# Causal scores by 64x64 tiles of the PE array, with the state update and the way of x^T moved

## The chip, the cores and the metric

The kernel runs on one core of a Trainium2 chip. The metric is the device time of one execution in microseconds (us), the median of several runs. TensorE (PE) multiplies matrices, VectorE (DVE) and ScalarE (ACT) work element by element, GpSimd (POOL) does the masking, and SyncE (SP) issues the DMA transfers. Matmuls write to PSUM, everything else lives in SBUF.

## What is computed

A gated linear attention (outer-product state with a forget gate) is followed by a multiplicative feed-forward network:

```python
batch, n_heads, seq, head_dim = (4, 8, 768, 48)
n_tokens, d_model, d_ff = (3072, 384, 1024)

f = 1.0 / (1.0 + np.exp(-f_logit))
for t in range(S):
    state = f[:, :, t, :, None] * state + np.einsum('bhd,bhe->bhde', k[:, :, t], v[:, :, t])
    y[:, :, t] = np.einsum('bhd,bhde->bhe', q[:, :, t], state)
x = y.transpose(0, 2, 1, 3).reshape(B * S, H * D)
a = x @ w1
b = x @ w2
out = ((a * b) @ w3) @ w_out
```

All inputs and the output are float32 except the weights, which arrive as 64-bit words and are converted on the chip.

## The kernel before

The sequence is cut into 24 units of 128 tokens (six for each of the four batches), each with all eight heads. For a unit, products of gates are built by scans on VectorE, so that with Q = q times the product of the gates from the unit's start and K = k times its reciprocal, the scores of a head are K^T Q, and everything before the unit comes through a state of 48x48 per head. Heads are stored in pairs: partitions 0 to 47 hold one head of a pair (`par` = 0), partitions 64 to 111 the other, and `hp` counts the four pairs. Six blocks of 512 tokens (four units each) then go through the feed-forward network (FFN). Here w3 and w_out are first folded into one matrix (L999), and the FFN products are made with seven instead of eight block products from the second block on (L542). A scheduler in the kernel (`Plan`) books each task with an estimated cost and emits the instructions of all engines in the order of the plan.

The tasks of one unit that the change touches, cut to their core. The pairs, their way out of PSUM, and the causal mask:

```python
def pairs():
    s["pa"] = ps.tile([P, 2, NQ], F32, name="pa")
    for hp in range(HP):                       # HP = 4, C = P = 128, NQ = 512
        cols = slice(hp * C, hp * C + C)
        for par in range(2):
            nc.tensor.matmul(
                s["pa"][:, par, cols], lhsT=s["K"][rows(par), cols], rhs=s["Q"][rows(par), cols],
                start=True, stop=True,
            )
...
def taken():
    s["A"] = work.tile([P, 2, HP, C], F32, name="A")
    nc.scalar.copy(s["A"].rearrange("p r h c -> p r (h c)"), s["pa"])
...
def causal():
    a = s["A"].rearrange("p r h c -> p (r h) c")
    nc.gpsimd.affine_select(
        out=a, in_=a, pattern=[[0, H], [1, C]], compare_op=ALU.is_ge, fill=0.0, base=0,
        channel_multiplier=-1,
    )
```

The values (scores times v) and, in the same task, what the state gives (queries); the update of the state is a task of its own:

```python
def side(u, hp, par):                          # column half and block of a head's output
    if u < NPE:                                # NPE = 4: the first four units
        return par, hp
    return (par ^ 1 ^ hp & 1), 2 * par + hp // 2
...
def value():
    ...
    for hp in range(HP):
        for par in range(2):
            half, b = side(u, hp, par)
            ...
            nc.tensor.matmul(
                y_block(b)[64 * half : 64 * half + w], lhsT=s["v"][:, h * D : h * D + w],
                rhs=s["A"][:, par, hp], start=bank not in met_, stop=opens, skip_group_check=True,
            )
    if not opens:
        for hp in range(HP):
            ...
            for par in range(2):
                half, b = side(u, hp, par)
                nc.tensor.matmul(
                    y_block(b)[rows(half)], lhsT=sb[(u - 1) % 2][rows(par), hp, rows(par)],
                    rhs=s["Q"][rows(par), hp * C : hp * C + C], start=False, stop=True,
                    skip_group_check=True,
                )
...
def update():
    s["pd"] = ps.tile([P, HP, R], F32, name="pk")[0:R, :, 0:D]
    for hp in range(HP):
        for par in range(2):
            h = 2 * hp + par
            w = 64 if par == 0 else D
            nc.tensor.matmul(
                s["pd"][64 * par : 64 * par + w, hp], lhsT=s["kt"][:, hp, 64 * par : 64 * par + w],
                rhs=s["v"][:, h * D : h * D + D], start=True, stop=True,
            )
```

The output of a unit is copied to `ys` and brought into the layout that the FFN reads (x^T, features on partitions) by transfers from SBUF to SBUF, ten for a unit; the first four units use matmuls with a permutation instead:

```python
def gather():
    for h in range(H):
        half, b = side(u, h // 2, h % 2)
        for r, kc, at_, m in runs(h):
            a = half * 64 + at_
            nc.sync.dma_start(block_xt()[r : r + m, kc, cols], s["ys"][a : a + m, b])
...
t["z"] = t["x"] = moves(6.2, 197, 300, gather, [t["y"]] + before, n0 - 100)
```

`ys` has three buffers, and the transfers wait (`before`) until the block two earlier has been read.

Of the kernel before, what the change touches and what calls it, by code (L numbers as in the profile page):

```python
# [45 lines left out]
P = 128  # L46
C = 128
# [26 lines left out]
class Plan:  # L74


    def __init__(self):
        self.tasks = []
        self.slots = {}

    def slot(self, name, n):
        self.slots[name] = [n, []]

# [10 lines left out]
    def order(self):  # L94
# [5 lines left out]

        def start(t):

            waits = list(t["deps"])
            for name in t["takes"]:
                n, taken = self.slots[name]
                if len(taken) >= n:
                    waits += enders[id(taken[-n])]
            if any(d["end"] is None for d in waits):
                return None
            return max(  # L110
                [free.get(t["eng"], 0.0)] + [d["end"] + (d["lag"] + t["slack"] if d["eng"] != t["eng"] else 0.0) for d in waits]
            )

        while left:
            at, _, _, t = min(
                ((at, t["prio"], t["no"], t) for t in left if (at := start(t)) is not None), key=lambda x: x[:3]
            )
            t["at"], t["end"] = at, at + t["cost"]
            free[t["eng"]] = t["end"]
            for name in t["takes"]:  # L120
                self.slots[name][1].append(t)
            left.remove(t)
            done.append(t)
# [43 lines left out]

def side(u, hp, par):

    if u < NPE:  # L170
        return par, hp
    return (par ^ 1 ^ hp & 1), 2 * par + hp // 2
# [3 lines left out]
def ranged(ctx, tc, q, k, f_logit, v, w1, w2, w3, w_out, out, ident, w12, wc, left):  # L176
# [11 lines left out]
    one = ctx.enter_context(tc.tile_pool(name="one", bufs=1))  # L188
    ps = ctx.enter_context(tc.tile_pool(name="ps", bufs=1, space=PSUM))
    ps_f = ctx.enter_context(tc.tile_pool(name="ps_f", bufs=NF, space=PSUM))  # L190
# [4 lines left out]
    qs, ks, fs = ([keep.tile([R, NQ], F32, name=f"{nm}{i}") for i in range(n)] for nm, n in (("q", 3), ("k", 2), ("f", 2)))  # L195
    sb = [keep.tile([R, HP, R], F32, name=f"sb{i}") for i in range(2)]
# [33 lines left out]
    plan.slot("f", NF)  # L230
    plan.slot("a", 2)
    plan.slot("ab", 4)
    moving = plan.add("PE", 0.0, lambda: None, takes=["ab"], prio=-1e9)
    coming = plan.add("PE", 0.0, lambda: None, takes=["ab"], prio=-1e9)

    def idle(n):

        to = ps_f.tile([P, TB], F32, name="f")[:, 0:TH]
        for _ in range(n):
            nc.tensor.matmul(to, lhsT=floor[:, 0:P], rhs=floor[:, 0:TH], start=True, stop=True)  # L240
# [56 lines left out]
    def moves(issue, size, rate, emit, deps, prio, late=0.0):  # L297

        i = plan.add("SP", issue, emit, deps, prio, lag=0.6)
        return plan.add("DMA", size / rate, lambda: None, [i], prio, lag=1.3 + late)  # L300

    def attention(u):
        s, t = st[u], tk[u]
        opens, closes = u % NCH == 0, u % NCH == NCH - 1
        n0 = need(u)
        slack = 0.8 if u >= NPE else 0.0
# [15 lines left out]
        t["lf"] = moves(0.87, 197, 250, load(fu, f_logit), free(2, "g"), n0 - 30)  # L322
        t["lk"] = moves(0.87, 197, 250, load(ku, k), free(2, "k"), n0 - 29.5)
        t["lq"] = moves(0.87, 197, 250, load(qu, q), free(3, "q"), n0 - 29)

        def load_v():
            s["v"] = at(12288 + NQ, DM) if u == 3 else loads.tile([P, DM], F32, name="vt")
            nc.sync.dma_start(s["v"], v[u])

        t["lv"] = moves(0.45, 197, 320, load_v, [] if u == 3 else past(u, 4 if u in (4, 5, 6) else 3, "v", "s"), n0 - (28.2, 28.2, 28.2, 29.6, 27)[min(u, NPE)])  # L330
# [5 lines left out]
        if not opens:  # L336
            tk[u - 1]["d"]["deps"].append(t["g"])
# [31 lines left out]
        def scale_k():  # L369
            s["K"] = work.tile([R, NQ], F32, name="K")  # L370
            nc.vector.tensor_tensor(s["K"], ku, s["R"], ALU.mult)  # L371

        t["k"] = plan.add("DVE", 0.7, scale_k, [t["r"], t["lk"]] + past(u, 2, "a", "t"), n0)
# [3 lines left out]
        def pairs():  # L377
            s["pa"] = ps.tile([P, 2, NQ], F32, name="pa")
            for hp in range(HP):
                cols = slice(hp * C, hp * C + C)  # L380
                for par in range(2):
# [3 lines left out]
                    )  # L385

        t["a"] = plan.add("PE", 1.1, pairs, [t["q"], t["k"]] + past(u, 1, "y" if u > NPE else "m"), n0 - 1000, slack=slack)

        def taken():
            s["A"] = work.tile([P, 2, HP, C], F32, name="A")  # L390
            nc.scalar.copy(s["A"].rearrange("p r h c -> p r (h c)"), s["pa"])  # L391

        t["m"] = plan.add("ACT", 1.1, taken, [t["a"]] + past(u, 2, "v"), n0)

        def causal():
            a = s["A"].rearrange("p r h c -> p (r h) c")
            nc.gpsimd.affine_select(  # L397
                out=a, in_=a, pattern=[[0, H], [1, C]], compare_op=ALU.is_ge, fill=0.0, base=0,
                channel_multiplier=-1,
            )  # L400

        t["c"] = plan.add("POOL", 1.2, causal, [t["m"]], n0)

        if not closes:
            def turn():
                s["pk"] = ps.tile([P, HP, R], F32, name="pk")
                for hp in range(HP):
                    nc.tensor.transpose(  # L408
                        out=s["pk"][:, hp], in_=s["K"][:, hp * C : hp * C + C], identity=ident[0:R, 0:R]
                    )  # L410

            t["t"] = plan.add("PE", 0.45, turn, [t["k"]] + past(u, 1, "d"), n0 - 999, slack=slack)

# [6 lines left out]
        def value():  # L420
            if u < NPE:
                s["py"] = ps_f.tile([P, HP, C], F32, name="f")[0:R]
            else:
                s["py"] = ps.tile([P, 2, NQ], F32, name="pa")[0:R, :, 0 : 2 * C]
            met_ = set()
            for hp in range(HP):
                for par in range(2):
                    h = 2 * hp + par
                    half, b = side(u, hp, par)
                    w = 64 if half == 0 else D  # L430
                    bank = (half, 0 if u < NPE else par)
                    nc.tensor.matmul(  # L432
                        y_block(b)[64 * half : 64 * half + w], lhsT=s["v"][:, h * D : h * D + w],
                        rhs=s["A"][:, par, hp], start=bank not in met_, stop=opens, skip_group_check=True,
                    )
                    met_.add(bank)
            if not opens:
                for hp in range(HP):
                    if u < NPE:
                        nc.tensor.matmul(  # L440
                            y_block(hp), lhsT=sb[(u - 1) % 2][:, hp], rhs=s["Q"][:, hp * C : hp * C + C],
                            start=False, stop=True, skip_group_check=True,
                        )
                        continue
                    for par in range(2):
                        half, b = side(u, hp, par)
                        nc.tensor.matmul(  # L447
                            y_block(b)[rows(half)], lhsT=sb[(u - 1) % 2][rows(par), hp, rows(par)],
                            rhs=s["Q"][rows(par), hp * C : hp * C + C], start=False, stop=True,
                            skip_group_check=True,  # L450
                        )

        def y_block(b):
            return s["py"][:, b] if u < NPE else s["py"][:, b // 2, b % 2 * C : b % 2 * C + C]

        t["v"] = plan.add(
            "PE", 1.05 if opens else 2.1 if u < NPE else 1.6, value, [t["c"], t["lv"]] + past(u, 1, "y", "b"),
            n0 - 998, takes=["f"] if u < NPE else [], slack=slack,
        )

        if not closes:
            def update():
                s["pd"] = ps.tile([P, HP, R], F32, name="pk")[0:R, :, 0:D]
                for hp in range(HP):
                    for par in range(2):
                        h = 2 * hp + par
                        w = 64 if par == 0 else D
                        nc.tensor.matmul(  # L468
                            s["pd"][64 * par : 64 * par + w, hp], lhsT=s["kt"][:, hp, 64 * par : 64 * par + w],
                            rhs=s["v"][:, h * D : h * D + D], start=True, stop=True,  # L470
                        )

            t["s"] = plan.add("PE", 0.6, update, [t["e"], t["lv"]] + past(u, 1, "d"), n0 - 997, slack=slack)

# [11 lines left out]
            t["d"] = plan.add("DVE", 0.55 if opens else 0.9, state, [t["s"], t["l"]] + past(u, 2, "b"), n0)  # L486
# [7 lines left out]
        def outcome():  # L494
            s["ys"] = work3.tile([R, HP, C], F32, name="ys")
            ys = s["ys"] if u < NPE else s["ys"].rearrange("p (r b) c -> p r (b c)", r=2)
            nc.scalar.activation(ys, s["py"], AF.Copy, accum_out=ysum[:, u : u + 1])  # L497

        t["y"] = plan.add(
            "ACT", 0.8, outcome, [t["v"]] + past(u, 3, "z"), n0 - 10, frees=[t["v"]] if u < NPE else [],  # L500
# [10 lines left out]
        def gather():  # L511
            for h in range(H):
# [909 lines left out]
```

## Time and profile before

| | |
|---|---|
| time, median of 3 runs | 506.15 us (505.76 to 507.29) |
| span of the profiled execution | 502.6 us |
| instructions | 8896 |
| granted TensorE clock, mean share | 0.998 |
| moved by DMA | 46.02 MB, 92 GB/s on average |

The span can be read as stages. The first 35 us bring up the first four units. From 35 to 76 us the first FFN block runs, from 76 to 130 us the eight folds of w3 and w_out beside the attention. From 130 to 345 us attention and FFN alternate on TensorE, and from 345 us on there is only FFN. In the table of the costliest groups of the page, each line gives the source line, engine, operation, output and inputs, tile rows by columns, moving shape, count, busy time and mean duration. The mean duration of a matmul has the length of its pipeline in it, so the cost of a matmul in a stream is the distance from its start to the next one's start.

Busy times of the engines by stage, as the trace gives them for stretches of the span:

```
us            PE busy   DVE busy   ACT busy   DMA share
0:35          35.00     30.85      22.86      0.85
35:76         41.00     38.65      24.82      0.64
76:130        54.00     52.57      27.96      0.47
130:182       52.00     43.84      21.96      0.38
307:345       38.00     18.71      10.54      0.14
375:502      120.88     69.31      11.37      0.08
```

### The profile page before, as it was taken

The numbers are of one execution on the slowest core, as the hardware profiler recorded it, in microseconds if no ns is written. First come the engines' busy times: TensorE is split into PE (matmuls) and PEld (weight loads), VectorE is DVE, ScalarE is ACT, GpSimd is POOL, SyncE is SP. The second block draws the span as 40 slices with busy tenths as digits, with TensorE's granted clock in tenths as the row PEclk, the third lists the DMA queues.
The fourth block names the chain that finished last, engine by engine and source line by source line (L and its number), as shares of the span: only waits on it lengthen the run. The fifth ranks groups of instructions, "written<-read, shape, count | busy, mean of one in ns | idle before, by whom it ended". The sixth has DMA issues, their size and how long they took to land.

```text
span 502.6 us, 8896 instructions
## 1 busy us (share of the span) xinstructions
PE 492.0 (98%) x3378; PEld 411.0 (82%) x3378; DVE 362.7 (72%) x701; ACT 161.6 (32%) x340; POOL 45.3 (9%) x51
## 2 busy tenths in 40 slices
PE   8899999999999999999999999999999999999995
PEld 6788645666798887889888899888889888889994
DVE  7998999999999868876588666445563777664541
ACT  4697455843344344432242112231010101011000
POOL 9210000101100021011111001000000000000000
PEclk9999999999999999999999999999999999999999
DMA  6996477642244434221151001110012100000011
GB/s 181 297 358 218 140 257 259 218 116 61 62 120 118 132 112 134 83 87 47 43 175 31 1 10 46 47 43 2 0 24 61 45 0 1 0 1 0 33 54 47
DMA packets 31027, 46.02 MB, mean 92 GB/s; under 512 B 6656, under 2 KB 20480, under 8 KB 29952
## 3 DMA queue, kind: packets, MB, share of 16 engines
q1 hardware_dynamic: 30976, 45.38, 29.1%
q8 instruction: 28, 0.46, 0.4%
q14 instruction: 23, 0.19, 0.1%
HBM read 36.70 MB, written 4.72 MB: 82 GB/s over the span
## 4 chain that ended last, share of the span: by engine, by line
PE 93%; DVE 3%; issue 1%; POOL 1%; DMA 0%; ACT 0%; SPq 0%; DVEq 0%; ACTq 0%; POOLq 0%
PE f L542 68%; PE f L999 8%; PE pa L382 5%; PE pa L432 4%; PE pk L468 2%; PE pa L447 2%; PE pk L408 2%; PE f L521 1%; DVE fwd L341 1%; DVE bwd L363 1%; PE f L440 1%; PE f L432 1%; DVE K L371 0%; DMA f<-in_f_logit_dram 0%; DVE Q L357 0%
## 5 line engine op out<-in xcount | busy, mean ns | idle before, releaser
L542 PE MATMUL f<-xt,w 128*128 128x256 f32 (+1 forms) x600 | 160.3, 397 | 0.0
L542 PEld LDWEIGHTS f<-xt,w 128*128 128x128 f32 x600 | 112.8, 190 | 25.0 <-issue 10.9
L542 PE MATMUL f<-place 128*128 128x192 f32 (+1 forms) x504 | 114.0, 351 | 0.0
L542 PEld LDWEIGHTS f<-place 128*128 128x128 f32 x504 | 87.4, 190 | 6.3 <-issue 0.6
L397 POOL TENSOR_SCALAR_AFFINE_SELECT A<-A 128x1024 f32<-128x1024 f32 x24 | 34.1, 1420 | 295.0 <-ACT A L391 295.0
L999 PE MATMUL f<-place 128*128 128x384 f32 x128 | 42.9, 490 | 0.0
L542 PE MATMUL f<-xt,place 128*128 128x256 f32 x144 | 37.7, 384 | 0.0
L999 PEld LDWEIGHTS f<-place 128*128 128x128 f32 x128 | 23.8, 190 | 16.0 <-issue 0.5
L645 ACT COPY a<-f 128x256 f32<-128x256 f32 x36 | 13.4, 372 | 70.8 <-PE f L542 56.7
L542 PE MATMUL f<-wc,ab 128*128 128x192 f32 x192 | 35.3, 327 | 0.0
L391 ACT COPY A<-pa 128x1024 f32<-128x1024 f32 x24 | 24.3, 1012 | 27.2 <-PE pa L382 27.2
L341 DVE TENSOR_TENSOR_SCAN fwd<-gate,floor 112x512 f32<-112x512 f32 x24 | 31.0, 1293 | 2.5 <-ACT gate L333 1.7
L542 PEld LDWEIGHTS f<-wc,ab 128*128 128x128 f32 x192 | 32.0, 190 | 0.7 <-issue 0.2
L669 DVE TENSOR_TENSOR place<-f,a 128x256 f32<-128x256 f32 x36 | 15.2, 423 | 21.5 <-PE f L542 21.3
L363 DVE TENSOR_TENSOR_SCAN bwd<-gate,back 112x512 f32<-112x512 f32 x24 | 29.4, 1225 | 0.7
L542 PEld LDWEIGHTS f<-xt,place 128*128 128x128 f32 x144 | 26.5, 189 | 4.0 <-DVE place L669 0.2
L382 PEld LDWEIGHTS pa<-Q,K 48*128 48x128 f32 x384 | 23.3, 187 | 7.4 <-issue 5.8
L382 PE MATMUL pa<-Q,K 48*128 48x128 f32 x384 | 27.9, 285 | 0.0
L357 DVE TENSOR_TENSOR Q<-q,fwd 112x512 f32<-112x512 f32 x23 | 18.7, 812 | 9.5 <-PE pa L447 9.5
L497 ACT ACTIVATE ys<-pa 112x512 f32<-112x512 f32 x20 | 12.0, 598 | 35.6 <-PE pa L447 18.1
L432 PEld LDWEIGHTS pa<-A,vt 128*48 128x48 f32 x320 | 17.1, 129 | 6.8 <-issue 6.1
L935 ACT ACTIVATE place<-place 128x512 f32<-128x512 f32 (+2 forms) x24 | 21.4, 890 | 3.4 <-DVE w L952 2.0
(110 smaller groups left out, 633.5 us busy)
## 6 DMA issues: line engine op xcount, KB each, us to landing
place<-in_w_dram SPq DMA_DIRECT2D x8, 1024.0 KB, 4.9
place<-in_w_dram SPq DMA_DIRECT2D x12, 512.0 KB, 9.5
out_dram<-o SPq DMA_DIRECT2D x24, 192.0 KB, 2.1
q<-in_q_dram SPq DMA_DIRECT2D x46, 96.0 KB, 2.4
vt<-in_v_dram SPq DMA_DIRECT2D x23, 192.0 KB, 2.8
f<-in_f_logit_dram SPq DMA_DIRECT2D x44, 96.0 KB, 2.3
k<-in_k_dram SPq DMA_DIRECT2D x44, 96.0 KB, 2.4
place<-in_w_out_dram SPq DMA_DIRECT2D x4, 768.0 KB, 5.1
```

The costliest lines, as they stand in the source:

```text
L341: nc.vector.tensor_tensor_scan(s["P"], gate[u % 2][:, 0:NQ], floor, 0.0, ALU.mult, ALU.max)
L357: nc.vector.tensor_tensor(s["Q"], qu, s["P"], ALU.mult)
L363: nc.vector.tensor_tensor_scan(s["R"][:, ::-1], gate[u % 2][:, NQ:0:-1], back[:, ::-1], 0.0, ALU.mult, ALU.max)
L382: nc.tensor.matmul(s["pa"][:, par, cols], lhsT=s["K"][rows(par), cols], rhs=s["Q"][rows(par), cols], start=True, stop=True,)
L391: nc.scalar.copy(s["A"].rearrange("p r h c -> p r (h c)"), s["pa"])
L397: nc.gpsimd.affine_select(out=a, in_=a, pattern=[[0, H], [1, C]], compare_op=ALU.is_ge, fill=0.0, base=0, channel_multiplier=-1,)
L432: nc.tensor.matmul(y_block(b)[64 * half : 64 * half + w], lhsT=s["v"][:, h * D : h * D + w], rhs=s["A"][:, par, hp], start=bank not in met ...
L542: nc.tensor.matmul(out_, lhsT=lhs[i], rhs=rhs[i], start=start and i == 0, stop=i == len(lhs) - 1, skip_group_check=True,)
L645: nc.scalar.copy(q["a"], q["X"])
L669: nc.vector.tensor_tensor(ups["u3", k], q["Y"], q["a"], ALU.add)
L935: nc.scalar.activation(m, hi.bitcast(F32), AF.Abs)
L999: nc.tensor.matmul(w3s["p", jc], lhsT=w3s[jc][:, kc * P : kc * P + P], rhs=wos[:, kc], start=(kc == 0), stop=(kc == KF - 1),)
```

## The change

The change does five things. All but the last concern the units from number 4 on.

1. **Pairs by 64x64 tiles.** A key after a query gives a score that the mask removes. Each head's 128x128 scores are now made in two pieces: the 64 early keys against all 128 queries, and the 64 late keys against the 64 late queries; the corner of late keys and early queries is not computed. For the second head pair of each two, the two halves of K are stored swapped, so that four matmuls at a time fall on the four 64x64 tiles of the array. v is loaded with its halves swapped for these heads, in three transfers instead of one; ScalarE copies the scores in three pieces, and GpSimd masks in four.
2. **The update beside the values.** Values, update and queries are one task, in this order, so values and update share one tile shape. The task waits for the turned K, the mask and the state.
3. **x^T by way of memory.** Two transfers write `ys` to a buffer in DRAM, and one reads it back in the layout of the FFN. For this each half of the partitions holds heads 0 to 3 or 4 to 7, and the heads are taken in the order 0, 2, 1, 3 of `hp`.
4. **Transfers in the schedule.** The plan books each transfer by itself and allows eight at a time (`lane`).
5. **PSUM banks.** The five banks of the FFN are given out by the plan to whoever can start earliest, instead of in turn.

The diff, cut to its core:

```diff
-    plan.slot("f", NF)
+    plan.pool("f", NF)
     plan.slot("a", 2)
+    plan.slot("lane", 8)
...
+def heads_of(u):
+    return range(HP) if u < NPE else (0, 2, 1, 3)
 def side(u, hp, par):
     if u < NPE:
         return par, hp
-    return (par ^ 1 ^ hp & 1), 2 * par + hp // 2
+    return hp // 2, 2 * par + hp % 2
...
+    def moves(n, size, rate, emit, deps, prio, late=0.0):
+        for j in range(n):
+            i = plan.add("SP", 0.45, (lambda: None) if j else emit, [d] if j else deps, prio - j * 1e-3, takes=["lane"], lag=0.6)
+            d = i
+            t = plan.add("DMA", size / n / rate, lambda: None, [i], prio - j * 1e-3, lag=1.3 + late, frees=[i])
+        return t
+
+    def loaded(dst, u):
+        if u < NPE:
+            nc.sync.dma_start(dst, v[u])
+            return
+        to, of = (t.rearrange("p (b two m) -> p b two m", two=2, m=2 * D) for t in (dst, v[u]))
+        nc.sync.dma_start(to[:, :, 0], of[:, :, 0])
+        for a in (0, 64):
+            nc.sync.dma_start(to[a : a + 64, :, 1], of[64 - a : P - a, :, 1])
...
+            kk, k_, r_ = (
+                x.rearrange("p (b two h c) -> p b two h c", two=2, h=2, c=C // 2) for x in (s["K"], ku, s["R"])
+            )
+            nc.vector.tensor_tensor(kk[:, :, 0], k_[:, :, 0], r_[:, :, 0], ALU.mult)
+            nc.vector.tensor_tensor(kk[:, :, 1, ::-1], k_[:, :, 1], r_[:, :, 1], ALU.mult)
...
+        for hp in range(0, HP, 2):
+            for late in range(2):
+                for swap in range(2):
+                    a = (hp + swap) * C
+                    h0 = 64 * (late ^ swap)
+                    for par in range(2):
+                        nc.tensor.matmul(
+                            s["pa"][h0 : h0 + 64, par, a + 64 * late : a + C],
+                            lhsT=s["K"][rows(par), a + h0 : a + h0 + 64],
+                            rhs=s["Q"][rows(par), a + 64 * late : a + C], start=True, stop=True,
+                        )
...
+            for p0, p1, f in ((0, P, slice(1, 4, 2)), (0, 64, slice(0, 1)), (64, P, slice(2, 3))):
+                nc.scalar.copy(...[p0:p1, :, f], ...[p0:p1, :, f])
-        t["m"] = plan.add("ACT", 1.1, taken, ...)
+        t["m"] = plan.add("ACT", 1.1 if u < NPE else 1.5, taken, ...)
...
+            for p0, f in ((0, 0), (0, 3), (64, 1), (64, 2)):
+                select(a[p0 : p0 + 64, :, f], [[0, HP], [1, C // 2]])
-        t["c"] = plan.add("POOL", 1.2, causal, [t["m"]], n0)
+        t["c"] = plan.add("POOL", 1.2 if u < NPE else 1.9, causal, [t["m"]], n0)
...
-        t["v"] = plan.add(
-            "PE", 1.05 if opens else 2.1 if u < NPE else 1.6, value, [t["c"], t["lv"]] + past(u, 1, "y", "b"), ...
-            t["s"] = plan.add("PE", 0.6, update, [t["e"], t["lv"]] + past(u, 1, "d"), n0 - 997, slack=slack)
+            t["a"] = plan.add("PE", 1.0, lambda: pairs(u), ...)
+            def value():
+                values(u)
+                if not closes:
+                    update(u)
+                from_state(u)
+            t["v"] = t["s"] = plan.add(
+                "PE", 1.2 + 0.35 * (not closes) + 0.5 * (not opens), value,
+                [t["c"], t["lv"]] + past(u, 0, "e") + past(u, 1, "y", "b", "d"), n0 - 998, slack=0.8,
+            )
...
-        def gather():
-            for h in range(H):
-                half, b = side(u, h // 2, h % 2)
-                for r, kc, at_, m in runs(h):
-                    a = half * 64 + at_
-                    nc.sync.dma_start(block_xt()[r : r + m, kc, cols], s["ys"][a : a + m, b])
+        def written():
+            s["yt"] = dram.tile([DM, C], F32, name="yt")
+            for half in range(2):
+                to = s["yt"][half * DH : half * DH + DH].rearrange("(b d) c -> d b c", d=D)
+                nc.sync.dma_start(to, s["ys"][rows(half)])
+
+        def gathered():
+            nc.sync.dma_start(block_xt()[:, :, cols], s["yt"].rearrange("(k p) c -> p k c", p=P))
...
-            t["z"] = t["x"] = moves(6.2, 197, 300, gather, [t["y"]] + before, n0 - 100)
+            t["z"] = moves(2, 197, 250, written, [t["y"]], n0 - 100)
+            t["x"] = moves(1, 197, 250, gathered, [t["z"]] + before, n0 - 100)
```

## The prediction

> **What bounds the kernel now.** I began with the busy times and the slices of the page.
>
> ```profile
> PE 492.0 (98%) x3378; PEld 411.0 (82%) x3378; DVE 362.7 (72%) x701; ACT 161.6 (32%) x340; POOL 45.3 (9%) x51
> ...
> PE   8899999999999999999999999999999999999995
> ...
> DVE  7998999999999868876588666445563777664541
> ...
> DMA  6996477642244434221151001110012100000011
> ```
>
> TensorE is occupied for 98% of the span, in every slice but the first two and the last. A busy TensorE need not be at its peak, so next came the chain that ended last.
>
> ```profile
> PE 93%; DVE 3%; issue 1%; POOL 1%; DMA 0%; ACT 0%; SPq 0%; DVEq 0%; ACTq 0%; POOLq 0%
> PE f L542 68%; PE f L999 8%; PE pa L382 5%; PE pa L432 4%; PE pk L468 2%; PE pa L447 2%; PE pk L408 2%; PE f L521 1%; DVE fwd L341 1%; DVE bwd L363 1%; PE f L440 1%; PE f L432 1%; DVE K L371 0%; DMA f<-in_f_logit_dram 0%; DVE Q L357 0%
> ```
>
> The other engines hold it only in the first 19 us (the scans of the first units). After 35 us TensorE never starves. I took the start-to-start distances of its single instructions: the FFN and fold matmuls (L542, L999) after 35 us sum to 383 us at their own pace (216 ns for 256 columns, 163 for 192, 323 for 384), and real waits add only four pieces: 0.35 us at 188.5 (values for their mask), 0.29 at 253.1, 0.81 at 375.6 (the final judgement) and 0.61 at 493.3, 2.1 us in all. So time can be had only from what the attention costs TensorE. Its pieces stand in the TensorE timeline; columns are start, length with the pipeline's tail, line, tiles, shape, count (start to start is the cost):
>
> ```profile
> 192.47 1.16 PE L382 MATMUL pa<-Q,K 48*128 48x128 f32 x16
> 193.63 0.70 PE L542 MATMUL f<-xt,place 128*128 128x256 f32 x2
> ...
> 207.82 1.09 PE L432 MATMUL pa<-A,vt 128*48 128x128 f32 x16
> 208.85 0.66 PE L447 MATMUL pa<-Q,sb 48*48 48x128 f32 x16
> 209.43 0.67 PE L468 MATMUL pk<-vt,kt 128*64 128x48 f32 x16
> 210.03 0.70 PE L542 MATMUL f<-xt,place 128*128 128x256 f32 x2
> ```
>
> Pairs cost 1.09 us, values 1.02, queries of the state 0.585, update 0.595. The counts are twice those in the code (8 matmuls of pairs give x16): each f32 matmul is two passes.
>
> And where values and update already stand side by side (a unit that opens a sequence, with no state to query):
>
> ```profile
> 189.07 1.09 PE L432 MATMUL pa<-A,vt 128*48 128x128 f32 x16 [0.19 <-POOL A L397]
> 189.99 0.64 PE L468 MATMUL pk<-vt,kt 128*48 128x48 f32 x16
> 190.55 0.48 PE L542 MATMUL f<-xt,w 128*128 128x256 f32 x1
> ```
>
> Here values take 0.91, update 0.56: the join without a change of tile shape is cheaper by 0.11.
>
> [...] An FFN matmul before pairs or values takes 309 ns to the next start instead of 216 (+93); the first pass in a new shape lasts longer (+30 for values, +20 to 40 for queries, +101 for pairs); the last adds +93; and the FFN matmul after it takes 320 (+104). In the update the 48- and 64-column tiles run at 45 and 58 ns each, out of step.
> [...]
> [...] The change keeps parity as the bank; the 48x48 queries already run four tiles at 109 ns for 128 columns.
> [...] So x^T pays two landings in series; in this trace one takes 1.8 us.
>
> **The change part by part**, for the 20 units from number 4 on; the first four keep their code.
>
> *Pairs.* Eight matmuls (two row tiles, 128 weight columns) become 16 on four 64x64 tiles. For two head pairs: two passes of 128 columns at 109 (as the queries' quads) and two of 64 at about 58 (weight-bound, as the 64-column update). Twice that is 0.67 us; with 0.03 for the first pass and 0.09 to drain, 0.79 against 1.09. But 64 loads and matmuls in 0.67 us are one per 10 ns; the tightest this trace shows is the queries' 32 in 0.436, one per 13.6. At that pace the stream takes 0.87, the piece 1.0, which is also the cost that the new schedule books. I choose the middle, 0.90: 20 x 0.19 = 3.8 us saved (1.8 to 6).
>
> *Values, update, queries.* Now: 17 x 1.61 + 3 x 0.91 + 13 x 0.595 + 3 x 0.564 = 39.5, and three updates stand between two FFN matmuls at 0.2 extra, together 40.1. After, for the 13 middle units: values 0.911, update 8 x 0.058 = 0.464, switch 0.123, queries 0.436, drain 0.093 = 2.03; three opening units 1.475 and four closing ones 1.61 as now: 37.2, a saving of 2.9. Against it stands the new order of heads: the two column halves no longer alternate with each matmul, but go two and two. If the tiles queue deeply enough, that is free; if the second half starts one pass late, it costs 0.11 x 20 = 2.2. The new schedule books 1.2 for values (1.05 before), so I take half: 2.9 - 1.1 = 1.8 us saved.
>
> *Off the path.* ACT copies the scores in three pieces instead of one of 1.01 us: about 0.60 + 0.37 + 0.37 by its 512- and 256-element copies. GpSimd masks in four ops instead of one (1.09 to 2.11, median 1.29): an estimated 1.6 to 2. K is scaled by two DVE ops of 256 (0.42 each) instead of one of 0.70. The way from scores to values grows by about 1 us, DVE by 0.14 us a unit. Units come every 10 us or more and the FFN fills, so this costs nothing unless a wait like that at 188.5 grows. The SyncE queue issues 10 transfers of 0.59 us for x^T and one of 0.37 for v now; after, two writes and one read, and three for v: some 3 us of issue less per unit. This removes waits of ACT, not of TensorE (view of the waits; total us, times, longest):
>
> ```profile
> ACT ys L497 <- DMA xt<-ys: 14.7, 4, 5.2
> ```
>
> Those keep the last outputs back to 373.7, and through them the judgement, TensorE's 0.81. Written to memory, ys comes free without a block buffer: that wait may go, and choosing PSUM banks by the earliest free may take another. I book 0.8 us.
>
> Sum: 3.8 + 1.8 + 0.8 = 6.4 us of 506.15, so 499.8.
>
> **The rivals.**
> *A limit of dispatch eats the tiles.* If 16 small matmuls and their loads cost what 8 larger ones do, pairs save nothing, and values in the two-and-two order lose 2 us: 504 to 506. For it: the new schedule's own costs (1.0 and 1.2), and no stream so dense in this trace. Against it: four queries start 7 ns apart.
> *A new wait on TensorE.* The update now waits for the mask as well. In this trace it often ran before its unit's values (174.9 against 189.07). State, blocks and the next values now hang in a row: about 2 + 0.9 + 0.75 us at ten or more per unit. It should hold; between 76 and 182 us, where DVE is busy for 97% and then 84% of the time, a slip of 1 us per unit over six units would give 505 to 507.
> *The full gain.* Pairs at 0.79, order free, waits gone: 6.0 + 2.9 + 1.5 = 10.4, so 495.8.
> *The transfers matter by themselves.* SyncE and DMA are hardly on the chain, so the new route and the eight lanes are worth about nothing; only the 35 us of start, where TensorE waits for the first units, could move by 1 us either way.
>
> **Range and chances.** The dispatch rival and the full gain span 495.8 to 506. I hold 495.5 to 504.5 at 8 in 10. Faster by over 2% means below 496.0, the full gain and a little luck: 0.10. Slower by over 2% would need 16 us of new waits on an engine that has 2 now: 0.03. Within 2%: 0.87.
>
> **What would show it.** In the TensorE timeline a pairs piece should take 0.8 to 1.0 us from its first start to the FFN's next; values-update-queries 2.03 (2.14 if the order costs). The FFN sum must stay at 383. ACT's wait for x^T should vanish and the judgement's wait shrink. The prediction is wrong if pairs take 1.09 or more, if values take over 1.2, if TensorE shows gaps of more than 3 us after 35, or if the first FFN matmul starts more than 1 us away from 35.1.

## The result, and the profile after

The changed kernel takes 499.14 us (median of 4 runs, 499.04 to 499.23), the kernel before 505.95 us beside it: a ratio of 0.9863, with a 95% interval of 0.9841 to 0.9885. The prediction was 499.8 us. The sum came out near; the terms are not all right, and errors offset each other.

The page of the kernel after, the same parts as shown of before (busy times, slices, the chain by engine and line):

```profile
PE 484.9 (98%) x3698; PEld 407.6 (82%) x3698; DVE 362.1 (73%) x721; ACT 166.8 (34%) x380; POOL 69.7 (14%) x115
...
PE   8889999999999999999999999999999999999995
...
DVE  7998899989989677878677965446673667664541
...
DMA  6889377563335554344532203100021000000011
...
PE 76%; POOL 1%; DVE 0%; ACT 0%; issue 0%
PE f L685 61%; PE pa L490 4%; PE f L1143 3%; PE pa L457 3%; PE pa L509 2%; PE pk L467 2%; PE pk L522 1%; POOL A L548 0%; ACT ys L635 0%; DVE place L949 0%; DVE o L970 0%; POOL A L560 0%; POOL A L559 0%; DVE nil L1202 0%; DVE zero L1200 0%
```

TensorE is still occupied for 98%; what shrank is its busy time, by 7.1 us. GpSimd holds 1% of the chain, as before; new is that the mask (L548) and two clearings (L559, L560) stand among its lines. The chain covers only 77% of the span this time, so for TensorE I rely on the distances between the starts of its instructions.

Two places of the TensorE timeline after, where pairs, and then values, update and queries stand between FFN work (start, length with the pipeline's tail, line, tiles, shape, count):

```profile
209.04 0.90 PE L457 MATMUL pa<-Q,K 48*64 48x128 f32 x32
209.87 0.60 PE L467 MATMUL pk<-ident,K 112*128 112x112 f32 x4
...
215.16 1.13 PE L490 MATMUL pa<-A,vt 128*64 128x128 f32 x16
216.09 0.61 PE L522 MATMUL pk<-vt,kt 128*64 128x48 f32 x16
216.63 0.65 PE L509 MATMUL pa<-Q,sb 48*48 48x128 f32 x16
217.22 0.59 PE L685 MATMUL f<-wc,ab 128*128 128x192 f32 x2
```

Start to start, a pairs piece costs 0.83 us (1.09 before). Values, update and queries cost 0.925 + 0.544 + 0.584 = 2.05 us in one block (2.20 before, in up to three places).

The ledger over the two profiled executions, all from start-to-start distances; their spans are 502.6 and 497.2, 5.4 apart. A wait is counted from the end of the step that TensorE takes anyway; where a change of tile shape follows, that step is 309 ns and not 216, so the prediction's waits of 0.35 and 0.29 us are 0.26 and 0.20:

| | before | after | gain |
|---|---|---|---|
| FFN and folds at their own pace, after 35 us | 383.5 | 383.5 | 0 |
| pairs, 20 units | 21.84 | 16.58 | +5.3 |
| values, update, queries, 20 units, with the changes of shape around lone updates | 40.1 | 37.7 | +2.4 |
| real waits of TensorE after 35 us | 1.9 | 3.0 | -1.1 |
| first FFN matmul starts at | 35.09 | 36.66 | -1.6 |

That is 5.0 of the 5.4 us. The medians are 6.8 apart because the profiled execution of the kernel before took 504.4 us, 1.6 below its median; what its longer executions lose no trace shows.

### The profile page after: what moved, and what is told of

Same layout as the page of the kernel before. It is cut to its first block, busy times and chain, and to the rows that moved or that the text cites. A ratio compares the mean times of both kernels' runs of the same rounds, so it can differ in the third digit from the quotient of the medians.

```text
span 497.2 us, 9542 instructions
## 1 busy us (share of the span) xinstructions
PE 484.9 (98%) x3698; PEld 407.6 (82%) x3698; DVE 362.1 (73%) x721; ACT 166.8 (34%) x380; POOL 69.7 (14%) x115
## 4 chain that ended last, share of the span: by engine, by line
PE 76%; POOL 1%; DVE 0%; ACT 0%; issue 0%
PE f L685 61%; PE pa L490 4%; PE f L1143 3%; PE pa L457 3%; PE pa L509 2%; PE pk L467 2%; PE pk L522 1%; POOL A L548 0%; ACT ys L635 0%; DVE place L949 0%; DVE o L970 0%; POOL A L560 0%; POOL A L559 0%; DVE nil L1202 0%; DVE zero L1200 0%
## 5 line engine op out<-in xcount | busy, mean ns | idle before, releaser
L685 PE MATMUL f<-xt,w 128*128 128x256 f32 (+1 forms) x600 | 158.5, 396 | 0.0
L685 PE MATMUL f<-place 128*128 128x192 f32 (+1 forms) x504 | 112.6, 350 | 0.0
L548 POOL TENSOR_SCALAR_AFFINE_SELECT A<-A 64x256 f32<-64x256 f32 (+1 forms) x84 | 57.2, 701 | 239.2 <-PE pk L467 104.3
L685 PE MATMUL f<-xt,place 128*128 128x256 f32 x144 | 37.7, 385 | 0.0
L394 DVE TENSOR_TENSOR_SCAN fwd<-gate,floor 112x512 f32<-112x512 f32 x24 | 29.7, 1237 | 2.6 <-ACT gate L386 2.1
L542 ACT COPY A<-pa 64x256 f32<-64x256 f32 (+1 forms) x60 | 24.3, 439 | 13.9 <-PE pa L457 13.3
L490 PEld LDWEIGHTS pa<-A,vt 128*64 128x64 f32 (+1 forms) x320 | 17.6, 129 | 7.8 <-issue 5.5
L490 PE MATMUL pa<-A,vt 128*64 128x128 f32 (+1 forms) x320 | 22.7, 280 | 1.0 <-POOL A L560 1.0
L685 PE MATMUL f<-place,w 128*128 128x256 f32 x72 | 21.6, 382 | 0.0
L1082 ACT ACTIVATE place<-place 128x512 f32<-128x512 uint32 (+2 forms) x24 | 21.1, 885 | 0.0
```

Of the source, the lines that this page charges most:

```text
L394: nc.vector.tensor_tensor_scan(s["P"], gate[u % 2][:, 0:NQ], floor, 0.0, ALU.mult, ALU.max)
L490: nc.tensor.matmul(y_block(u, b)[64 * half : 64 * half + w], lhsT=s["v"][:, h * D : h * D + w], rhs=s["A"][:, par, hp], start=zone not in ...
L542: nc.scalar.copy(parts_of(s["A"].rearrange("p r h c -> p (r h c)"))[p0:p1, :, f], parts_of(s["pa"].rearrange("p r n -> p (r n)"))[p0:p1, : ...
L548: nc.gpsimd.affine_select(out=a, in_=a, pattern=pattern, compare_op=ALU.is_ge, fill=0.0, base=0, channel_multiplier=-1,)
L685: nc.tensor.matmul(out_, lhsT=lhs[i], rhs=rhs[i], start=start and i == 0, stop=i == len(lhs) - 1, skip_group_check=True,)
L1082: nc.scalar.activation(lo.bitcast(F32), lo, AF.Copy, bias=2.0, scale=2.0**-51)
```

## The experiments

All but one start from the changed kernel. Each ratio is to the kernel before on the same chip.

**1. The pairs alone undone.**

```diff
-        if u < NPE:                 # pairs by 64x64 tiles from unit 4 on
+        if True:                    # whole 128x128 scores from two row tiles
             for hp in range(HP):
                 cols = slice(hp * C, hp * C + C)
```

with the scores copied in one piece, masked by one op, and K and v unswapped.

> The changed kernel with only the pairs undone (whole 128x128 scores from two row tiles, one copy, one mask, v and K unswapped), the order of tasks held. If the pairs carry the gain: a pairs piece takes 1.09 us again instead of 0.83, 20 x 0.26 = 5.3 us back, less about 1 us because the single mask ends earlier in the two units where TensorE now waits for GpSimd: 503.3 us (502.5 to 504.6). If the gain comes from the schedule, the transfers or the joined task: within 1 us of 499.1.

Measured: 504.26 us (503.96 to 504.39), ratio 0.9957 (0.994 to 0.9974). TensorE's timeline of this run:

```profile
210.50 1.16 PE L445 MATMUL pa<-Q,K 48*128 48x128 f32 x16
211.59 0.60 PE L467 MATMUL pk<-ident,K 112*128 112x112 f32 x4
```

The pairs pieces are at 1.09 us again, and the values' waits for GpSimd are gone; three waits of the FFN for VectorE came (0.20 to 0.25 us each). So the pairs carry most of the gain, and not the new order, which is the same here.

**2. The corner left out without swapping halves.**

```diff
-                    h0 = 64 * (late ^ swap)     # late keys in the other column half for every second head pair
+                    h0 = 64 * late              # early keys left, late keys right, for all
```

> The corner is left out as in the changed kernel, but no halves are swapped: early keys always on the left 64 columns (128 queries), late keys always on the right (64 queries), v by one transfer, K by one op. If the stream of the fuller column half sets the time: 8 passes of 109 ns, 1.03 us per pairs piece, about 4 us slower than the changed kernel, 503.2 us (502 to 504). If four tiles at once or fewer computed scores are enough: 0.83 us per piece and 499 us.

Measured: 506.35 us (504.7 to 506.76), ratio 0.9996 (0.9983 to 1.0009). TensorE's timeline of this run, at the first pairs and the first values after 35 us:

```profile
88.76 1.09 PE L456 MATMUL pa<-Q,K 48*64 48x128 f32 x32
89.78 0.60 PE L466 MATMUL pk<-ident,K 112*128 112x112 f32 x4
...
98.03 1.59 PE L489 MATMUL pa<-A,vt 128*64 128x128 f32 x16 [2.47 <-POOL A L559]
99.39 1.03 PE L521 MATMUL pk<-vt,kt 128*64 128x48 f32 x16
```

The pairs piece takes 1.02 us, as expected: the left column half streams 128 queries for every head while the right one streams 64, and the fuller half sets the time. Twenty pieces at 0.193 more make 3.9 us. The rest of the loss is the values' wait for GpSimd, read with the next run, and slower passes after it: the values last 1.35 us until the update starts instead of 0.925, and until 101.9 us this costs some 2 us (last section).

**3. The corner computed.**

```diff
-                            s["pa"][h0 : h0 + 64, par, a + 64 * late : a + C],
+                            s["pa"][h0 : h0 + 64, par, a : a + C],
...
-                            rhs=s["Q"][rows(par), a + 64 * late : a + C], ...
+                            rhs=s["Q"][rows(par), a : a + C], ...
```

> Four 64x64 tiles as in the changed kernel, but the corner is computed as well (late keys against all 128 queries; its result is not read). If streaming sets the time: 4 quads of two passes at 109 ns, 1.03 us per pairs piece, 503.2 us (502.5 to 504). If dispatch of 32 passes sets it: 0.83 to 0.86 us per piece, within 0.7 us of 499.1.

Measured: 506.68 us (504.9 to 507.23), ratio 1.0009 (0.9998 to 1.002). TensorE's timeline of this run:

```profile
89.29 1.10 PE L457 MATMUL pa<-Q,K 48*64 48x128 f32 x32
90.33 0.51 PE L467 MATMUL pk<-ident,K 112*128 112x112 f32 x3
```

1.035 us a piece: 0.206 more for 4 passes per tile of 64 columns more, 51 ns each. So streaming sets the time, and not dispatch, which rules out the first rival. It also says what the tiles are good for: four 64x64 tiles by themselves (1.035) are hardly better than two row tiles of 128 weight columns (1.092). The gain is the corner that smaller tiles allow to leave out, and it comes through only if both column halves get the same work (run 2).

Twenty pieces at 0.206 make 4.1 us; the spans of the profiled executions are 6.4 apart. (The median lies 1.3 us above the profiled execution, and no trace shows why.) Most of the rest is GpSimd. Its timeline in the kernel after, where the values first wait, and in this run, each with VectorE's op at its first mask op. The two MEMSETs clear the corner that no matmul fills now; they are needed in units 4 and 5 alone, since the two tiles of A are then used again and again:

```profile
91.28 1.42 DVE L1096 CUSTOM_DVE_ANT_0 place<-place 128x2048 uint16<-128x2048 uint16 x1
...
91.21 4.51 POOL L548 TENSOR_SCALAR_AFFINE_SELECT A<-A 64x256 f32<-64x256 f32 x4 [61.10 <-issue]
95.78 0.31 POOL L559 MEMSET A<- 64x256 f32 x1
96.12 0.31 POOL L560 MEMSET A<- 64x256 f32 x1
...
105.84 3.90 POOL L548 TENSOR_SCALAR_AFFINE_SELECT A<-A 64x256 f32<-64x256 f32 x4 [9.42 <-ACT A L542]
```

```profile
91.36 1.23 DVE L1096 CUSTOM_DVE_ANT_0 place<-place 128x2048 uint16<-128x2048 uint16 x1
...
91.50 6.57 POOL L548 TENSOR_SCALAR_AFFINE_SELECT A<-A 64x256 f32<-64x256 f32 x4 [61.31 <-issue]
98.12 0.31 POOL L559 MEMSET A<- 64x256 f32 x1
98.47 0.31 POOL L560 MEMSET A<- 64x256 f32 x1
...
108.40 3.71 POOL L548 TENSOR_SCALAR_AFFINE_SELECT A<-A 64x256 f32<-64x256 f32 x4 [9.62 <-ACT A L542]
```

The same four ops take 4.5 us in one run and 6.6 in the other, where they start 0.3 us later beside the same VectorE work. In the kernel after, the first of the four starts 0.07 us ahead of VectorE's op and takes 0.41 us; in this run VectorE is 0.14 us ahead, and the first takes 1.36. The values wait 0.73 us in the first and 2.8 in the second. An op of this size takes 0.41 us at best; here they took up to 1.87 and 2.51. VectorE is busy for 94% of this stage (76 to 130 us), with the weights' conversion and the scans. It goes the other way round too: a VectorE product of 4 columns that takes 0.15 us elsewhere took 1.07 beside a mask op of 1.09 us, in the start of the kernel after (24.28 us). The two engines were slower beside each other; by what, no run isolates.

**4. The update after the queries.**

```diff
                 values(u)
+                from_state(u)
                 if not closes:
                     update(u)
-                from_state(u)
```

> The one task in the order values, queries, update, so that values and update no longer share a tile shape side by side. If the saved change of shape is the gain of the join: 2.20 us instead of 2.05 for the three in 13 middle units, 13 x 0.15 = 2.0 us slower than the changed kernel, 501.1 us (500.5 to 501.7). If the order is free and only the common task counts: 499.1 within 0.5.

Measured: 501.48 us (501.26 to 501.62), ratio 0.9904 (0.9887 to 0.992). The TensorE timeline of this run:

```profile
204.64 1.13 PE L490 MATMUL pa<-A,vt 128*64 128x128 f32 x16
205.70 0.65 PE L509 MATMUL pa<-Q,sb 48*48 48x128 f32 x16
206.29 0.67 PE L522 MATMUL pk<-vt,kt 128*64 128x48 f32 x16
206.88 1.13 PE L685 MATMUL f<-xt,place 128*128 128x256 f32 x4
```

2.24 us instead of 2.05, with one change of tile shape more; 13 units by 0.19 make 2.4, and the time grew by 2.3. So the order pays, and not the common task. The change from values to queries is dearer than in the kernel before (values last 1.06 until the queries start, 1.02 before), which is why this block is above the 2.20 of before. The new order of heads is the likely reason; no run isolates it.

**5. and 6. x^T by ten transfers again**, first booked as ten in the eight lanes, then as one task of 6.2 us outside them, as before the change.

```diff
-            t["z"] = moves(2, 197, 250, written, [t["y"]], n0 - 100)
-            t["x"] = moves(1, 197, 250, gathered, [t["z"]] + before, n0 - 100)
+            t["z"] = t["x"] = moves(10, 197, 300, gather, [t["y"]] + before, n0 - 100)          # run 5
+            i = plan.add("SP", 6.2, gather, [t["y"]] + before, n0 - 100, lag=0.6)               # run 6
+            t["z"] = t["x"] = plan.add("DMA", 197 / 300, lambda: None, [i], n0 - 100, lag=1.3)
```

> The changed kernel with x^T brought over by ten transfers from SBUF to SBUF again, booked as ten. If transfers are off the path of TensorE: 499.1 within 1.2 us either way (a new order of tasks can move the waits for GpSimd), with ScalarE's waits for x^T back in the waits. If the way by memory is worth something by itself: 501.5 us or more, with gaps in TensorE's FFN stream.

Measured: 518.09 us (517.45 to 519.41), ratio 1.0246 (1.0209 to 1.0282). My theory falls: I had the transfers off the path.

> As the run with x^T by ten transfers (518.1 us), but booked in the plan as the kernel before booked them: one task of 6.2 us on SyncE, outside the eight lanes. If the loss came from booking them as ten in the lanes: 499 to 501 us. If it comes from the SyncE queue itself, where ten transfers that wait for a block buffer hold the loads behind them: 510 us or more, with gaps of TensorE before and after 250 us and a late judgement.

Measured: 508.16 us (505.36 to 510.04), ratio 1.0034 (1.0012 to 1.0057). Both readings hold a part: ten of the 19 us came with that booking, nine remain. (With another booking the plan's order of tasks can move too; it was not held.) Where the nine arise is seen in run 6, in the timelines of SyncE, ScalarE and TensorE (what an engine waited for stands at the line's end):

```profile
170.81 6.30 SPq L680 DMA_DIRECT2D xt<-ys  x10
177.21 0.53 SPq L982 DMA_DIRECT2D out_dram<-o  x1
177.83 0.84 SPq L361 DMA_DIRECT2D f<-in_f_logit_dram  x2
...
181.51 0.63 ACT L386 ACTIVATE gate<-f 112x512 f32<-112x512 f32 x1 [4.20 <-DMA f<-in_f_logit_dram]
...
183.81 0.38 ACT L795 COPY a<-f 128x256 f32<-128x256 f32 x1
...
184.24 1.13 PE L692 MATMUL f<-xt,w 128*128 128x256 f32 x4 [2.73 <-ACT a L795]
```

Ten issues hold SyncE for 6.3 us; the load of f, behind them, comes late; ScalarE's next op, the gate, waits 4.2 us for it, and behind the gate stands the copy that TensorE's FFN needs: 2.73 us of TensorE. Three more such waits follow, of 2.13 us at 205.5, 1.28 at 257.6 and 1.15 at 261.2, each behind work of VectorE or ScalarE that was late for x^T or for a load of f. With 1.7 us of slower passes after one of them (last section) they make 9.0 of the 9.8 us between the profiled spans of this run and of the kernel after. With v now in three transfers, SyncE would need about 11 us a unit for issues (6.3 for x^T, 2.7 for f, k and q, 1.9 for v), and units come every 10 to 12. By way of memory x^T takes about 1.4.

**7. The kernel before with only x^T by way of memory**, four writes and one read for a unit.

```diff
-            t["z"] = t["x"] = moves(6.2, 197, 300, gather, [t["y"]] + before, n0 - 100)
+            t["z"] = moves(1.8, 197, 250, written, [t["y"]], n0 - 100)
+            t["x"] = moves(0.45, 197, 250, gathered, [t["z"]] + before, n0 - 100)
```

> The kernel before with only x^T by way of memory (four writes and one read for a unit). If transfers are off TensorE's path there: 505.8 us within 1, ScalarE's waits for x^T gone, the wait for the judgement near 0.5 instead of 0.8. If the way by memory is a gain of its own: under 504.

Measured: 503.98 us (503.42 to 505.74), ratio 0.9974 (0.9963 to 0.9986): 1.5 us below the 505.48 of the kernel before beside it, at the edge of my second case. ScalarE's waits for x^T are gone. The wait for the judgement (a small matmul that tests, late in the kernel, whether the products of gates stayed in range, and that waits for VectorE) fell from 0.81 to 0.34, and the waits for the mask and ahead of a lone update went; two waits of the folds came, 0.35 and 0.44 us at 76 and 82. The profiled executions of the two kernels are equally long (spans 502.7 and 502.6 us), so where the 1.5 us of the medians arise is not shown. So the route is a small gain by itself and a condition for the rest.

**8. Any number of transfers at a time in the plan** (`takes=["lane"]` removed).

> The changed kernel with any number of transfers at a time in the plan. The first FFN matmul starts 1.57 us later in the changed kernel than before. If the lanes changed the order of the start: it starts near 35.1 us again instead of 36.7 and the time is about 497.6 us. If not: the start stays at 36.7, 499.1 within 0.7.

Measured: 499.92 us (499.43 to 500.06), ratio 0.9881 (0.985 to 0.9912), and the first FFN matmul at 36.85. The lanes are not what moved the start. The time is 0.8 us above the changed kernel's, but the intervals of the two ratios overlap, so no gain of theirs is shown.

**9. The fillers ahead of unit 3's values removed.** The kernel keeps TensorE going in the start with idle matmuls wherever the plan sees a hole before 35 us. The TensorE timeline of the kernel after:

```profile
28.19 0.55 PE L467 MATMUL pk<-ident,K 112*128 112x112 f32 x4
30.14 1.13 PE L277 MATMUL f<-floor 112*128 112x256 f32 x4 [1.41 <-ACT ys L635]
31.21 1.09 PE L490 MATMUL f<-A,place 128*64 128x128 f32 x16
```

The mask of these values was ready at 30.1. The fillers write a PSUM bank that the plan had given to unit 2's output, wait for ScalarE to read it, and then take 1.06 us ahead of values that could start.

```diff
-FULL = 35.0
+FULL = 20.0
```

> The changed kernel without the two filler matmuls ahead of unit 3's values (they wait for ScalarE to read the PSUM bank they write, and hold the values that were ready). If these fillers are part of the later start: the first FFN matmul at 35.6 instead of 36.7 us, 498.1 us (497.7 to 498.5). If another wait ends last there: no change, 499.1.

Measured: 498.14 us (498.1 to 498.31), ratio 0.9846 (0.9815 to 0.9877), first FFN matmul at 35.58. As expected.

**10. The start in the order of before as well**: unit 3's K turned before unit 2's values.

```diff
+            if u == NPE - 1:
+                tk[u - 1]["v"]["deps"].append(t["t"])
```

> The changed kernel with the start in the order of before (unit 3's K is turned before unit 2's values) and without the two filler matmuls ahead of unit 3's values. Fillers alone gave 498.1 and a first FFN matmul at 35.6. If the turn that came late costs as well (the update of unit 3 then fills a wait instead of standing between the last permutations): first FFN matmul at 34.0 to 34.7, 497.0 us (496.4 to 497.6). If not: 498.1 again.

Measured: 497.48 us (497.43 to 497.81), ratio 0.9837 (0.9806 to 0.9869). FFN work starts at 33.40, with one permutation of 1.34 us among it, which comes to 34.7. Of the 0.8 us won there, 0.5 is lost again at 75.6, where the folds now wait, and 0.3 comes back at 81, where their wait shrinks from 0.74 to 0.43. Late turn and fillers explain the later start; why the plan chose that order was not settled (run 8 excludes the lanes).

**11. The mask in three ops of 512 elements** that clear the corner too.

```diff
-            for p0, f in ((0, 0), (0, 3), (64, 1), (64, 2)):
-                select(a[p0 : p0 + 64, :, f], [[0, HP], [1, C // 2]])
-            if u < NPE + 2:
-                nc.gpsimd.memset(a[0:64, :, 2], 0.0)
-                nc.gpsimd.memset(a[64:P, :, 0], 0.0)
+            select(h[:, 0::2], [[0, HP], [1, C]])               # heads that are not swapped
+            # and two ops of 64x512 for the swapped ones, base -64 and 0
```

> The mask by three ops of 512 elements that also clear the corner, instead of four of 256 and two clearings. If each GpSimd op pays for the VectorE work beside it, fewer ops end sooner: the waits of values for GpSimd in the fold stage (0.73 and 0.42 us, 2.6 to 2.9 in the two runs with slower pairs) fall under 0.3 together, 498.1 us (497.6 to 498.7). If only the amount of data counts: three ops take as long as four, and the time stays at 499.1 or grows.

Measured: 499.5 us (499.1 to 499.65), ratio 0.9873 (0.9842 to 0.9904). The values' waits in the fold stage went as expected, and the time did not: three waits of the FFN for VectorE appeared (0.20, 0.35 and 0.40 us at 246, 278 and 289). At 276 us two of the longer mask ops ran for 2.13 us beside a scan that took 1.49 instead of 1.22. At 246 and 289 too, products of VectorE that take 0.42 us elsewhere took 0.84 and 0.85 beside a mask op. What GpSimd no longer lost, VectorE lost.

**12. Run 10 with the corner cleared early**, as a task of its own as soon as the units two earlier have been read.

```diff
-            if u < NPE + 2:
-                nc.gpsimd.memset(a[0:64, :, 2], 0.0)
-                nc.gpsimd.memset(a[64:P, :, 0], 0.0)
+            t["w"] = plan.add("POOL", 0.7, corner, past(u, 2, "v"), n0 - 50)
```

> The run e13_start with the corner cleared ahead of the scores in units 4 and 5, instead of after the mask. The values waited for these clearings 0.73 and 0.42 us. If nothing else ends there: 1.0 us faster than e13_start, 496.0 us (495.5 to 496.6). If the freed time is taken by a wait elsewhere, as with the mask in three: the same as e13_start.

Measured: 496.15 us (495.97 to 496.23), ratio 0.9808 (0.9777 to 0.984): 1.3 us on run 10. The first view is of TensorE's waits in the kernel after, the second in this run:

```profile
PE f L277 <- ACT ys L635: 1.4, 1, 1.4
PE pa L490 <- POOL A L560: 1.0, 2, 0.7
PE pk L467 <- DVE K L425: 1.0, 2, 0.8
```

```profile
PE f L277 <- DVE floor L297: 1.7, 1, 1.7
PE pk L467 <- DVE K L425: 0.7, 1, 0.7
PE pk L522 <- ACT kt L571: 0.5, 1, 0.5
```

The wait for GpSimd's last clearing (L560) is gone (that for ScalarE went with the fillers, run 9). The two clearings, 0.6 us after the last mask op, were the part of GpSimd's delay that TensorE felt. This version beats both kernels.

## Why the prediction was right or wrong

*The bound* was right: the FFN's own sum is 383.5 us in both kernels, and 5.0 of the 5.4 us between the profiled executions are found in the attention's pieces, TensorE's waits and the start.

*Pairs*: the pace of the passes was right (109 and 58 ns for 128 and 64 columns taken, 109 and 56 to 58 found between 209.2 and 209.7 us of the kernel after) and the size was off: 0.83 us a piece where I chose 0.90, so 5.3 us saved instead of 3.8. The failed term is the half allowance for dispatch, "one per 13.6" ns. Run 3 shows that streaming sets the piece; the working without the allowance gave 0.79, and the other 0.04 lies in the changes of shape (the first pass lasts 51 ns longer and the last adds 111, at 209.04 and 209.70 us, where 30 and 93 were taken).

*Values, update, queries*: 2.4 us saved against 1.8. The allowance for heads taken two and two, 0.055 us a unit, was too large: values take 0.925 before an update where 0.911 was worked out, and 0.04 more in closing units. The saved change of shape is shown by run 4.

*Off the path* failed twice. "An estimated 1.6 to 2" for the masks was 3.3 to 4.5 in the fold stage, since the ops' times were read where they ran as one and not beside a VectorE without gaps; this and the clearings after them, which I left out, cost 1.15 us where I said "this costs nothing". And I booked 0.8 us of waits gone; they grew by 1.1. The judgement's wait shrank as said (0.81 to 0.46), and the wait at 188.5 went, but a wait for a PSUM bank of the folds came (0.74 at 82.8). No run isolates the new choice of PSUM banks, the fifth part of the change.

*The start* was given 1 us either way; it moved by 1.6, and by the prediction's own sign (more than 1 us from 35.1) that part was wrong. Two fillers behind a PSUM bank and the late turn explain it (runs 9 and 10).

*The transfers*: "worth about nothing" was wrong. I read only who waited for a DMA. Run 6 shows a queue that delays ScalarE, which delays TensorE; with the other parts of the change in place, the old route costs nine us, and in the kernel before the new one gains 1.5 by the medians.

So pairs and the joined task brought 2.1 us more than said, waits and start 3.5 less: the profiled executions show 5.0 us where the sum said 6.4. The medians are 6.8 apart, since the kernel before was profiled in an execution 1.6 us under its median; that the median came out within 0.7 us of the prediction is in part luck.

## What to carry to other kernels

Small PE tiles paid here by the work that they allowed to leave out (0.83 us a pairs piece, 1.035 with the corner computed), and only with equal streams in the two column halves (1.02 without); put pieces with the same tile shape side by side (2.05 us a block here, 2.24 otherwise). When a mask or a copy is cut into more ops, read its time in the stage where VectorE is busiest (the four mask ops took 3.3 to 4.5 us beside a VectorE busy for 94%, and one takes 0.41 at best), and move what needs no input (clearings, fillers) out from behind it (1.3 us in run 12, 1.0 in run 9). A DMA queue without a single wait of the bound engine can still be a condition: add up its issue time per unit of work before putting more into it (here 11 us for units that come every 10 to 12, and 9 us lost).

## What was not expected of the hardware

A GpSimd select of 64x256 takes 0.41 us at best and up to 2.51 beside a busy VectorE, and with a start 0.3 us later four of them took 2.1 us longer.

After two of the waits seen here TensorE came back slower for a while. In run 6, after a wait of 2.13 us, eight passes from 206.7 us on took 427 ns instead of 216:

```profile
202.34 1.03 PE L692 MATMUL f<-xt,w 128*128 128x256 f32 x4
205.50 0.70 PE L692 MATMUL f<-place 128*128 128x256 f32 x2 [2.13 <-DVE place L816]
206.03 2.98 PE L692 MATMUL f<-xt,w 128*128 128x256 f32 x8
208.81 1.67 PE L692 MATMUL f<-xt,place 128*128 128x256 f32 x4
```

Run 2 shows the same from 98.5 to 101.9 us, after a wait of 2.47 us. But the length of the wait alone does not decide it: after the wait of 2.73 us at 184.24 in run 6, and after another of 2.73 us in run 3, the passes kept their pace. What decides it no run isolates. So a wait here can cost more than its length: the eight slow passes add 1.7 us to the 2.13.
